# Half-size products in the third block from the end, and vector sums moved between stages, in a retention and bilinear FFN kernel

## The chip, the cores and the metric

The kernel runs on one core of a Trainium2 chip, as one launch. The time is the device time of that launch in microseconds; the kernel before takes 318.87 us (median of three runs). A core has five engines that run their own queues of instructions and wait for each other by semaphores: TensorE (PE, with its weight loads shown as PEld), VectorE (DVE), ScalarE (ACT), GpSimd (POOL) and SyncE (SP), which here only starts DMAs. Matmul results land in PSUM, in eight banks of 2 KB for each of 128 partitions; all else on the chip lies in SBUF.

## The reference

Eight batches of eight heads, 576 positions, head size 64: a retention layer (scores with a decay for each head, no softmax), then a bilinear feed-forward layer over all 4608 tokens.

```python
scores = scale * np.matmul(q, k.transpose(0, 1, 3, 2))
gamma = 1.0 - 2.0 ** (-5.0 - np.arange(H, dtype=np.float32))
Dmat = np.where(rel >= 0, gamma[:, None, None] ** rel[None, :, :], 0.0)
attn = np.matmul(scores * Dmat[None], v)
x = attn.transpose(0, 2, 1, 3).reshape(B * S, H * D)   # 4608 x 512
out = ((x @ w_a) * (x @ w_b)) @ w_out                  # 512 -> 1536 -> 512
```

## The kernel before

**Tokens and blocks.** Tokens are handled in 18 pairs of 256 (`NP`; n = 0 to 17) and the FFN in ten blocks that begin at tokens 0, 512, 768, 1024, 1536, 2048, 2560, 3072, 3584 and 4096 (the second and third hold 256, the rest 512, two pairs). Pairs 15 and 17 (`LEFT`) hold the last 64 positions of each batch; the others hold 256 positions of one batch.

**A block has two stages.** In the *layer*, x (transposed, `xT`, 128 partitions by 4 by 512 tokens) is multiplied with the weights w_a and w_b. The 1536 features are 12 rows F of 128. For each F, four matmuls of 512 columns make `pa` (L1387), ACT copies it to `ha` (L1398), four more make `pb` (L1405), and DVE multiplies both into `hT` (L1410). In the *rows* stage `hT` is multiplied with w_out into the output. From token 1536 on (`MIXED`) the rows stage (`rows_mixed`, tiles named `m`, L1045) takes two rows F at a time (a pair p of h rows, six in all) by seven half-size products instead of eight, in the manner of Strassen and Winograd. That needs sums of h rows (`row_sums`, L979, into `hsum` and in place into `hT`) and sums of w_out (`weight_sums`, made once), both on DVE. ACT copies the banks out (`straight`, `crossed`, L1057), POOL adds two of the four output quarters (L1068), and DVE makes `less` (L1078) and from it the other two (L1085), which are the last to read the banks of `m34`.

**Sevens in the layer too.** In the last block, pairs p = 0, 1, 3, 4 of h rows (`SEVENS`) are also taken by seven products in the layer, and in the block before it (3584, `MIDDLE`) pairs 0 and 1. One pair is then 28 matmuls of 256 columns instead of 16 of 512 (`layer_mixed`, L1220, tiles `lm`, `ls`, `la`). They need eight weight sums for p = 0 and 1 together, eight for p = 3 and 4 (`combine`, L1173, tiles `combos` and `combo`), and four sums of x for each block (`combine_rows`, L1190, tile `rows`). ACT copies products out (L1227), DVE adds (L1231), and POOL multiplies the a part with the b part into `hT` (L1232). `ORDER_MIDDLE` is the order of the products by hand; after it come F = 4 to 11 as usual.

**The retention in between.** PE's work is counted in units of one 512-column matmul (0.2155 us). A list `todo` says at which unit of the whole run other work is issued; it is looked at only at an edge, which in a usual layer is the end of each `pb`, and in a layer by sevens comes only when no pair of h rows is under way. A *stretch* (into, outof) issues on PE the key-value products (`kv`) and scores (`sc`) of one pair of tokens and the outputs (`o`, `os`) of the pair before. Two stretches stand in each later block, about 24 and 88 units into the layer. Ahead of them POOL casts and scales q, k, v of a pair (`ahead`, L578 to L615), SP transposes q and k by DMA (`turn`) and loads the pair after the next.

**What follows a stretch.** DVE adds `kv` to the running state in four sums (L690), which free the two banks of `kv`, and masks the scores (L743); ACT converts states and copies the outputs into x. Part of this goes into a list `jobs` with a priority and a cost. `work(budget)` issues from it after each `pb`. `flush` issues all jobs, `settle` only those of the states and masks. `NOW` is how many of the four state sums are issued at the stretch itself; the others are jobs. Row sums have priority 1, weight sums 1.5 and up.

**Banks and buffers.** `pa`, `pb`, `kv`, `os`, `lm` and part of `m` share the four banks of `ps_ffn`; a new tile takes the bank whose last reader comes first in program order. `ls` and `sc` share two banks, `la`, `o` and the rest of `m` two more (one tile). Output tiles `osb` have four buffers; `store_formed` issues the stores of a block's outputs at F = 2 of the next usual layer, or in the last layer.

**Places.** In the kernel before, the weight sums are issued as jobs: p = 0 with w_a in the layer of 2048, with w_b in that of 2560; p = 3 with w_a in that of 3072, with w_b in 3584 (50 units in). The x sums of the next block stand in the rows stage after both `less`.

Of the kernel before, what the change touches and what calls it, by code (L numbers as in the profile page):

```python
# [11 lines left out]
BF16 = mybir.dt.bfloat16  # L12
# [6 lines left out]
def kernel(  # L19
# [10 lines left out]
    nc = tc.nc  # L30
# [4 lines left out]
    NTOK = B * S  # L35
# [9 lines left out]
    NP = NTOK // 256  # L45
# [799 lines left out]

    def stretch(into, outof):

        (settle if into == NP - 1 else flush)()
        if into == FIRST:
            ps_next("pair", 2)  # L850
        if into in LEFT:
            open_outputs(outof, True)
            open_outputs(into)
            masked = matched(into)
            close_outputs(outof)
            later.append(lambda: masked(0))
            later.append(lambda: masked(1))
            return
        if into == 5:
            convert, convert_swapped = keyed(into, False,  # L860
                                             lambda: open_outputs(outof))
            pop()
            pop()
        else:
            if outof is not None and outof not in opened:
                open_outputs(outof)
            convert, convert_swapped = keyed(into, outof is None)
        masked = matched(into)
        if outof is not None:
            close_outputs(outof)  # L870
        if into == 4:
            later.append(later.pop(1))
            behind.extend([lambda: masked(0), convert, lambda: masked(1)])
            behind.extend(convert_swapped(apart=True))
            return
        if into > MIXED:
            for add in later[:NOW]:
                add()
            jobs.extend((0, 0.5, add) for add in later[NOW:4])
            jobs.append((0, 0, lambda: copies_due.extend(  # L880
                [convert, convert_swapped])))
            jobs.extend((0 if into % 2 else 2, 0.7,
                         lambda on=on: masked(on)) for on in (0, 1))
            copies_due.extend(later[4:])
            later.clear()
            return
        later.append(lambda: (convert(), masked(0)))
        later.append(lambda: (convert_swapped(), masked(1)))
# [116 lines left out]
    def rows_mixed(tok0, hT, sums):  # L1005
# [118 lines left out]
                yield from product(g, 1, part, g == 0)  # L1124
        work(math.inf)
        pass_on(math.inf)
        for g in (0, 1):
            yield from cross(g)
            lessen(g)
        if tok0 + 512 in MIDDLE or pair[1] == NP - 3:  # L1130
            for i in range(4):
                combine_rows(tok0 + 512, i)
        for g in (0, 1):
            for way, *end in ends:
                yield from product(g, way, range(NP2), False)
# [4 lines left out]

    SEVENS = (0, 1, 3, 4)
    COMMON = (0, 1)
    SHARED = 0
    combos = {}

# [3 lines left out]
            "p c (q e f) -> p e c q f", e=2, f=128)  # L1149
        return [[w[:, e, c:c + 2] for c in (0, 2)] for e in (0, 1)]  # L1150

    def combine(p, m, i):

        if (p, m) not in combos:
            shape = [128, 4, 2, 2, 128]
            if p in COMMON:
                if m == 0:
                    both = late["combo"].tile([128, 2] + shape[1:], BF16,
                                              tag="combo", name="combos")
                    combos[p, 0], combos[p, 1] = both[:, 0], both[:, 1]  # L1160
            else:
                combos[p, m] = stage.tile(shape, BF16, tag=("qf", "kf")[m],
                                          name="combo")
            for own in (0, 1):
                if (p, own) in combos:
                    combos[p + 1, own] = combos[p, own]
        (a11, a12), (a21, a22) = quarter_weights(m, p, 2)
        s3, s1, s2, s4 = (combos[p, m][:, k] for k in range(4))
        out, one, other, op = [(s3, a11, a21, ALU.subtract),
                               (s1, a21, a22, ALU.add),  # L1170
                               (s2, a22, s3, ALU.subtract),
                               (s4, a12, s2, ALU.subtract)][i]
        jobs.append((1.5 + i / 10, 0.5, lambda: nc.vector.tensor_tensor(  # L1173
            out, one, other, op=op)))

    row_combos = {}

# [76 lines left out]

        return quarter, after

    MIDDLE = (NTOK - 1024,)
    ORDER_MIDDLE = (
        (1, 0), (2, 0), (1, 1), (6, 0), (5, 0), (6, 1), (7, 0), (3, 0),
        (5, 1), (2, 1), (4, 0), ("a", 4), (3, 1), (7, 1), ("b", 4),  # L1260
# [4 lines left out]
    def middle_layer(tok0, xT, hT, sums):  # L1265

        quarter, after = layer_mixed(tok0, xT, hT)
        has, underway = {}, set()
        for way, at in ORDER_MIDDLE:
            if way in ("a", "b"):  # L1270
                F = at
                p1 = ps_ffn.tile([128, 512], FP32, tag="ab", name="p" + way)
                for c in range(NC):
                    w = wa_sb if way == "a" else wb_sb
                    nc.tensor.matmul(p1, w[:, c, F * 128:F * 128 + 128],  # L1275
                                     xT[:, c], start=(c == 0),
                                     stop=(c == NC - 1))
                    if c < NC - 1:
                        yield 1, False
                if way == "a":  # L1280
                    pop()
                    pass_on(1)
                    if F == 2:
                        store_formed()
                    has[F] = ha_pool.tile([128, 512], BF16, tag="ha",
                                          name="ha")
                    nc.scalar.copy(has[F], p1)
                    yield 1, False
                    continue
                nc.vector.tensor_tensor(hT[:, F], has[F], p1, op=ALU.mult)  # L1290
                pop()
                done, last = F // 2 if F % 2 else None, 1
            else:
                if way == 1:
                    underway.add(at)
                yield from quarter(at, way)
                after(at, way)
                if way == 4:
                    underway.remove(at)
                done, last = at if way == 4 else None, 0  # L1300
            if done is not None and done % 2:
                jobs.extend(row_sums(hT, sums, done - 1, done + 1))
            if done == 5:
                while later:
                    pop()
                work(math.inf, 1)
            work(SHARE_MIDDLE[way])
            yield last, way in ("b", 4) and not underway
# [298 lines left out]
    for n in range(8, NP, 2):  # L1607
# [19 lines left out]
             (411.95, store_held, (2,)), (412.3, load_pair, (11, (K, V))),  # L1627
             (458, load_pair, (12,)), (447, store_held, (2,)),
             (456, store_held, (2,))]
    NOW = 2  # L1630
    LATE = 8, 8, 8, 50, 8
    CAST_A, TURN_A, CAST_B, TURN_B = 96, 58, 96, 58
    for n in range(11, NP):
        casts[n] = placed[n] - (CAST_A if n % 2 else CAST_B)
        turns[n] = placed[n] - (TURN_A if n % 2 else TURN_B)
    for fn, places in ((ahead, casts), (turn, turns)):
        todo += [(at, fn, (n,)) for n, at in places.items()]
    for i in range(16):
        todo.append((starts[NP - 10 + 2 * (i // 4)] + LATE[i // 4]
                     + i % 4 * LATE[4], combine,  # L1640
                     (SEVENS[i // 8 * 2], i // 4 % 2, i % 4)))
    todo.sort(key=lambda e: e[0])

    at = 0.0
# [40 lines left out]
```

## Time and profile before

| | |
|---|---|
| runs | 318.87 us median of 3 (318.01 to 318.91) |
| profiled execution | 318.54 us, of which the span of its instructions is 316.8 |
| layer of block 1536 | 121.6 to 145.1 in the span |
| rows stage of 1536 | 145.1 to 154.4 |
| rows stage of 2048 | 178.6 to 187.9 |
| rows stage of 2560 | 211.9 to 221.1 |
| rows stage of 3072 | 244.2 to 253.2 |
| rows stage of 3584 | 275.2 to 284.2 |
| layer of 4096 | 284.2 to 303.7 |
| its rows stage and the end | 303.7 to 316.8 |

The profile is of one execution. In a timeline, a row gives the start in us from the span's start, the duration of the group, the engine, the line of the program, the operation, the tile that it writes and those that it reads, its shape and how many instructions are merged in the row; in brackets stands the idle time of the engine before the group and what ended it. Matmuls overlap, so that a group of four with 512 columns lasts 1.03 us though the next one can start 0.86 after it. Some matmul records are missing; a group then shows x3.

### The profile page before, as it was taken

Reading aid. Unit: us, or ns where it says so; the run is one execution under the profiler, and the core shown is the slowest. Engines: PE = TensorE matmul, PEld = TensorE weight load, DVE = VectorE, ACT = ScalarE, POOL = GpSimd, SP = SyncE. Lnnn points to the kernel's source line nnn. Section 1 sums busy time; section 2 is a strip of 40 time slices with the busy share of each in tenths; the row PEclk is TensorE's granted clock in tenths of the full one; section 3 lists DMA queues with packets and bytes.
Section 4 is the critical chain, followed back from the end, with each engine's and each line's share of the span. In section 5 each row is a group of like instructions: output and inputs, shape, how many; then the busy total and the mean of one; then the engine's idle time right before and its main releaser. Section 6 shows DMA issues by size and latency. Waiting matters only on the chain.

```text
span 316.8 us, 9373 instructions
## 1 busy us (share of the span) xinstructions
PE 306.2 (97%) x3836; PEld 191.1 (60%) x3871; DVE 218.7 (69%) x426; ACT 151.0 (48%) x339; POOL 169.6 (54%) x187
## 2 busy tenths in 40 slices
PE   8899999999999999999999999999999999999995
PEld 3554457768544554548654774468545875587774
DVE  5845346767857662579568957886678786859873
ACT  6745346526435454444455535444434555335630
POOL 3990068654994568574796069704990340035313
PEclk9999999999999999999999999999999999999999
DMA  8999999999999999999999986983730030004004
GB/s 213 257 203 207 253 231 194 184 211 179 208 178 222 212 216 204 231 223 280 197 256 218 178 218 139 187 185 77 191 59 11 2 132 2 2 0 134 1 3 132
DMA packets 144795, 50.94 MB, mean 161 GB/s; under 512 B 126576, under 2 KB 141680, under 8 KB 144752
## 3 DMA queue, kind: packets, MB, share of 16 engines
q1 hardware_dynamic: 138272, 45.10, 70.3%
q0 software_dynamic: 5808, 4.72, 9.5%
q8 instruction: 30, 0.49, 0.7%
q10 hardware_dynamic: 672, 0.52, 0.5%
q14 instruction: 13, 0.11, 0.1%
HBM read 37.75 MB, written 9.44 MB: 149 GB/s over the span
## 4 chain that ended last, share of the span: by engine, by line
PE 88%; DVE 3%; issue 2%; DMA 2%; SPq 2%; ACT 2%; DVEq 0%
PE pb L1405 21%; PE pa L1387 20%; PE m L1045 17%; PE po L1431 7%; PE lm L1220 3%; PE pa L1275 2%; PE pb L1275 2%; DMA qf<-in_q_dram 2%; SPq L182 2%; PE ls L1220 2%; PE po L931 2%; PE sc L734 1%; PE o L762 1%; PE o L775 1%; PE kv L663 1%
## 5 line engine op out<-in xcount | busy, mean ns | idle before, releaser
L1410 DVE TENSOR_TENSOR hT<-ha,pb 128x512 bf16<-128x512 bf16 (+1 forms) x96 | 59.3, 618 | 50.0 <-PE pb L1405 43.1
L1405 PE MATMUL pb<-xT,wb_sb 128*128 128x512 bf16 (+1 forms) x382 | 86.9, 352 | 1.0 <-DVE hT L1410 0.7
L1398 ACT CAST ha<-pa 128x512 bf16<-128x512 f32 (+1 forms) x96 | 50.9, 531 | 72.2 <-PE pa L1387 69.5
L1387 PE MATMUL pa<-xT,wa_sb 128*128 128x512 bf16 (+1 forms) x358 | 82.8, 351 | 1.8 <-issue 1.1
L1405 PEld LDWEIGHTS <-wb_sb 128*128 128x128 bf16 x384 | 37.4, 98 | 36.6 <-issue 2.1
L1387 PEld LDWEIGHTS <-wa_sb 128*128 128x128 bf16 x376 | 35.8, 98 | 32.7 <-issue 0.3
L1068 POOL TENSOR_TENSOR osb<-crossed,straight 128x512 f32<-128x512 f32 x12 | 15.2, 1269 | 73.3 <-ACT crossed L1057 53.9
L615 POOL TENSOR_TENSOR vb<-vf,vs 128x1024 bf16<-128x1024 f32 (+1 forms) x17 | 29.4, 1731 | 4.1 <-DMA vf<-in_v_dram 1.9
L578 POOL TENSOR_TENSOR qkb<-qf,qs 64x1024 bf16<-64x1024 f32 x12 | 23.3, 1941 | 15.4 <-DMA qf<-in_q_dram 15.4
L1045 PEld LDWEIGHTS <-hT 128*128 128x128 bf16 x288 | 28.1, 98 | 4.4
L1431 PE MATMUL po<-wo_sb,hT 128*128 128x512 bf16 x113 | 26.7, 379 | 0.8 <-issue 0.6
L583 POOL TENSOR_TENSOR qkb<-qf,qs 64x512 bf16<-64x512 f32 x24 | 25.4, 1077 | 0.7
L1045 PE MATMUL m<-wo_sums,hsum 128*128 128x256 bf16 x216 | 25.7, 273 | 0.0
L1045 PEld LDWEIGHTS <-hsum 128*128 128x128 bf16 x216 | 21.1, 98 | 2.4
L979 DVE TENSOR_TENSOR hsum<-hT 128x512 bf16<-128x512 bf16 (+2 forms) x51 | 22.1, 462 | 0.4
L690 DVE TENSOR_TENSOR sums<-kv,sums 128x256 f32<-128x256 f32 x44 | 18.6, 422 | 2.2 <-DVE sums L687 0.5
L743 DVE TENSOR_TENSOR sT<-sc,mask 128x512 bf16<-128x512 f32 x30 | 19.8, 682 | 0.0
L608 POOL CAST qkb<-kf 64x512 bf16<-64x512 f32 (+1 forms) x34 | 19.2, 592 | 0.9
L604 POOL CAST qkb<-kf 64x1024 bf16<-64x1024 f32 (+1 forms) x17 | 16.1, 945 | 6.1 <-DMA kf<-in_k_dram 5.3
L1431 PEld LDWEIGHTS <-hT 128*128 128x128 bf16 x120 | 11.2, 98 | 12.4
L1078 DVE TENSOR_TENSOR less<-m,crossed 128x512 f32<-128x512 f32 (+1 forms) x14 | 8.3, 613 | 13.2 <-ACT crossed L1057 13.2
L1045 PE MATMUL m<-wo_sums,hT 128*128 128x256 bf16 x144 | 16.9, 273 | 0.0
(159 smaller groups left out, 442.4 us busy)
## 6 DMA issues: line engine op xcount, KB each, us to landing
qf<-in_q_dram SPq DMA_DIRECT2D x32, 256.0 KB, 4.7
vf<-in_v_dram SPq DMA_DIRECT2D x32, 256.0 KB, 5.3
kf<-in_k_dram SPq DMA_DIRECT2D x31, 256.0 KB, 4.9
out_dram<-osb SPq DMA_DIRECT2D x9, 512.0 KB, 3.9
out_dram<-osb SPq DMA_DIRECT2D x22, 128.0 KB, 2.8
wo_sb<-in_moe_w_out_dram POOLq DMA_DIRECT2D x3, 512.0 KB, 16.1
out_dram<-osb SPq DMA_DIRECT2D x6, 256.0 KB, 3.7
qf<-in_q_dram SPq DMA_DIRECT2D x8, 128.0 KB, 3.7
```

The source lines that it names most:

```text
L578: nc.gpsimd.tensor_tensor(per_head(qkb[0:64, Q]), per_head(t[0:64]), by[0:64].unsqueeze(2).to_broadcast([64, 2 * H, D]), op=ALU.mult)
L583: nc.gpsimd.tensor_tensor(per_head(qkb[64:128, Q])[:, 1 - r::2], per_head(t[64:128])[:, r::2], by[64:128, r::2].unsqueeze(2).to_broadcast( ...
L608: nc.gpsimd.tensor_copy(to[:, :, 1 - r], fro[:, :, r])
L615: nc.gpsimd.tensor_tensor(vb[:, e].rearrange("p (h d) -> p h d", d=D), t[:, e].rearrange("p (h d) -> p h d", d=D), decay[:, at], op=ALU.mult)
L743: nc.vector.tensor_tensor(sT[:, on].rearrange("p c k s -> p (c k) s"), sc[on].rearrange("p c k s -> p (c k) s"), mask3.unsqueeze(1).to_bro ...
L979: lambda e=ways[i]: nc.vector.tensor_tensor(*e[:3], op=e[3]))
L1045: nc.tensor.matmul(to, rows, cols, start=(begins and p == 0), stop=True, skip_group_check=True)
L1387: nc.tensor.matmul(pa[:, 0:n], wa_sb[:, c, fs], xT[:, c], start=(c == 0), stop=(c == NC - 1))
L1398: nc.scalar.copy(ha[:, 0:n], pa[:, 0:n])
L1405: nc.tensor.matmul(pb[:, 0:n], wb_sb[:, c, fs], xT[:, c], start=(c == 0), stop=(c == NC - 1))
L1410: nc.vector.tensor_tensor(hT[:, F, 0:n], has[F][:, 0:n], pb[:, 0:n], op=ALU.mult)
L1431: nc.tensor.matmul(po, hT[:, F, u * 128:(u + 1) * 128], wo_sb[:, F], start=(F == 0), stop=(F == NF - 1))
```

## The change

- Block 3072 (`NTOK - 1536`) joins `MIDDLE`: its pairs 0 and 1 of h rows are taken by seven products in the layer. Its row sums are made in two groups (`GROUPS`), for pairs 0 to 3 and 4 to 5, as in a usual layer; those of 3584 stay in three.
- Weight sums: four are issued straight to DVE in the rows stage of block 1536 and four in that of 2048 (`between`, `AT`), between the products that need no `less` and the last ones; these are all of p = 0. The eight of p = 3 are jobs of block 3584, from 50 units on, eight units apart (`after_these`).
- The sums of x (`combine_rows`) are issued in that same place, ahead of `cross` and `less`; since 3072 is in `MIDDLE`, there are three sets of them instead of two.
- State sums: four at once at a stretch into an odd pair, one into an even pair (`NOW = 1, 4`), instead of two each.
- The stretch into pair 15 calls `settle` instead of `flush`, as the one into pair 17 did.
- The units of `todo` follow, since block 3072 now counts four units less.

```diff
-        (settle if into == NP - 1 else flush)()
+        (settle if into in LEFT else flush)()
...
         if into > MIXED:
-            for add in later[:NOW]:
+            now = NOW[into % 2]
+            for add in later[:now]:
                 add()
-            jobs.extend((0, 0.5, add) for add in later[NOW:4])
+            jobs.extend((0, 0.5, add) for add in later[now:4])
...
         work(math.inf)
         pass_on(math.inf)
+        if tok0 + 512 in MIDDLE or pair[1] == NP - 3:
+            for i in range(4):
+                combine_rows(tok0 + 512, i)
+        for sum_ in between.pop(tok0, ()):
+            combine(*sum_, now=True)
         for g in (0, 1):
             yield from cross(g)
             lessen(g)
-        if tok0 + 512 in MIDDLE or pair[1] == NP - 3:
-            for i in range(4):
-                combine_rows(tok0 + 512, i)
         for g in (0, 1):
             for way, *end in ends:
...
     COMMON = (0, 1)
+    EACH = [(p, m, i) for p in SEVENS[::2] for m in (0, 1) for i in range(4)]
+    AT = (4, 4, 0, 0, 0)
+    between, rest = {}, EACH[:]
+    for t, count in zip(range(256 * MIXED, NTOK - 512, 512), AT):
+        between[t], rest = rest[:count], rest[count:]
+    after_these = {t: [rest.pop(0) for _ in range(min(count, len(rest)))]
+                   for t, count in ((NTOK - 1536, 0), (NTOK - 1024, 8))}
...
-    def combine(p, m, i):
+    def combine(p, m, i, now=False):
...
             if p in COMMON:
-                if m == 0:
-                    both = late["combo"].tile([128, 2] + shape[1:], BF16,
-                                              tag="combo", name="combos")
-                    combos[p, 0], combos[p, 1] = both[:, 0], both[:, 1]
+                both = late["combo"].tile([128, 2] + shape[1:], BF16,
+                                          tag="combo", name="combos")
+                combos[p, 0], combos[p, 1] = both[:, 0], both[:, 1]
...
-        jobs.append((1.5 + i / 10, 0.5, lambda: nc.vector.tensor_tensor(
-            out, one, other, op=op)))
+        def made():
+            nc.vector.tensor_tensor(out, one, other, op=op)
+
+        if now:
+            made()
+        else:
+            jobs.append((1.5 + i / 10, 0.5, made))
...
-    MIDDLE = (NTOK - 1024,)
+    GROUPS = ((0, 4), (4, 6)), ((0, 2), (2, 4), (4, 6))
+    MIDDLE = (NTOK - 1536, NTOK - 1024)
...
-            if done is not None and done % 2:
-                jobs.extend(row_sums(hT, sums, done - 1, done + 1))
+            for p0, p1 in GROUPS[MIDDLE.index(tok0)]:
+                if done == p1 - 1:
+                    jobs.extend(row_sums(hT, sums, p0, p1))
...
-    NOW = 2
-    LATE = 8, 8, 8, 50, 8
+    NOW = 1, 4
+    LATE = 8, 50, 8
...
-    for i in range(16):
-        todo.append((starts[NP - 10 + 2 * (i // 4)] + LATE[i // 4]
-                     + i % 4 * LATE[4], combine,
-                     (SEVENS[i // 8 * 2], i // 4 % 2, i % 4)))
+    for t, sums_ in after_these.items():
+        todo += [(starts[t // 256] + LATE[t == NTOK - 1024] + LATE[2] * i,
+                  combine, sum_) for i, sum_ in enumerate(sums_)]
```

## The prediction, made before the changed kernel ran

> **What bounds the kernel now.** I read the page first, for the engines and the chain that ended last; then the stretches of the last blocks side by side; then TensorE's (PE's) timeline for holes; then what VectorE (DVE) and GpSimd (POOL) did around each hole.
>
> ```profile
> span 316.8 us, 9373 instructions
> PE 306.2 (97%) x3836; PEld 191.1 (60%) x3871; DVE 218.7 (69%) x426; ACT 151.0 (48%) x339; POOL 169.6 (54%) x187
> ```
>
> PE is busy 97% of the span, so a change pays only if PE has less to do or waits less. The stretches below are four layers (the first half of a block: x times w_a and w_b, then the product). Columns: length, then busy time and count for PE, weight load, DVE, ACT and POOL, then PE's granted clock.
>
> ```profile
> core 0: us, PE busy (x) PEld busy (x) DVE busy (x) ACT busy (x) POOL busy (x), PEclk, DMA share, GB/s
> 154.40:178.60 24.20, 23.46 (x343) 11.73 (x346) 17.89 (x30) 11.55 (x23) 16.82 (x15) 1.00 1.22 219
> 187.90:211.90 24.00, 23.24 (x342) 11.69 (x345) 19.00 (x30) 11.15 (x22) 15.54 (x14) 1.00 0.98 192
> 221.10:244.20 23.10, 22.78 (x311) 11.38 (x313) 17.14 (x26) 9.41 (x21) 15.81 (x14) 1.00 0.38 93
> 253.20:275.20 22.00, 21.84 (x280) 13.19 (x282) 16.89 (x36) 11.21 (x25) 4.24 (x6) 1.00 0.13 49
> ```
>
> They are the layers of blocks 2048, 2560, 3072 and 3584. The clock is 1.00 throughout. 3072 is the one that changes; 3584 already has two pairs of h rows by seven products, so it is the pattern. All four are PE-bound, but the first two are longer than their work. Where PE waited is seen in its timeline, where each group of four 512-column matmuls should start 0.86 after the one before:
>
> ```profile
> 131.52 1.03 PE L1387 MATMUL pa<-xT,wa_sb 128*128 128x512 bf16 x4
> 132.53 1.02 PE L1405 MATMUL pb<-xT,wb_sb 128*128 128x512 bf16 x4
> ...
> 162.55 1.03 PE L1387 MATMUL pa<-xT,wa_sb 128*128 128x512 bf16 x4
> 163.56 1.02 PE L1405 MATMUL pb<-xT,wb_sb 128*128 128x512 bf16 x4
> ...
> 171.33 1.03 PE L1387 MATMUL pa<-xT,wa_sb 128*128 128x512 bf16 x3
> 172.67 1.02 PE L1405 MATMUL pb<-xT,wb_sb 128*128 128x512 bf16 x4 [0.32 <-DVE hT L1410]
> ...
> 195.88 1.03 PE L1387 MATMUL pa<-xT,wa_sb 128*128 128x512 bf16 x4
> 197.29 1.02 PE L1405 MATMUL pb<-xT,wb_sb 128*128 128x512 bf16 x4 [0.39 <-DVE hT L1410]
> ```
>
> Start to start less 0.86 gives waits of 0.15, 0.15, 0.48 and 0.55, in all 1.33 us. Each is a pb that needs a PSUM bank which DVE's product hT has not freed. DVE's and then POOL's timeline tell why:
>
> ```profile
> 162.82 0.69 DVE L1410 TENSOR_TENSOR hT<-ha,pb 128x512 bf16<-128x512 bf16 x1 [1.00 <-PE pb L1405]
> ...
> 169.30 2.73 DVE L1173 TENSOR_TENSOR combos<-wa_sb,combos 128x512 bf16<-128x512 bf16 x2
> 171.95 0.67 DVE L1410 TENSOR_TENSOR hT<-ha,pb 128x512 bf16<-128x512 bf16 x1
> ...
> 193.69 2.09 DVE L1173 TENSOR_TENSOR combos<-wb_sb 128x512 bf16<-128x512 bf16 x1
> 196.56 0.68 DVE L1410 TENSOR_TENSOR hT<-ha,pb 128x512 bf16<-128x512 bf16 x1
> ```
>
> ```profile
> 193.60 1.90 POOL L615 TENSOR_TENSOR vb<-vf,vs 128x1024 bf16<-128x1024 f32 x1
> 195.46 2.08 POOL L578 TENSOR_TENSOR qkb<-qf,qs 64x1024 bf16<-64x1024 f32 x1
> ```
>
> The two long waits end with an hT that stood behind weight sums (L1173). Such a sum is held while POOL multiplies: the one at 193.69 ends at 195.78, 0.28 after POOL's product, though POOL's next product had come up at 195.46. The two short ones come just after a stretch: the state sums still hold the banks of kv, two sums made at once and two after the next hT, so the second pb gets the bank that hT (162.82 to 163.51) has just left.
>
> **The change part by part.** *Sevens in block 3072.* For pairs 0 and 1, 32 matmuls of 512 columns become 56 of 256. Their prices stand in the chain of waits, one run of each kind:
>
> ```profile
> 244.22 9.17 PE m L1045 x84
> ...
> 260.92 0.86 PE pa L1275 x4
> ```
>
> That is 0.109 each against 0.2155: 56 x 0.109 = 6.10 for 32 x 0.2155 = 6.90, so -0.80, all of it on PE, the engine that sets the end. The layer of 3584, where the same 56 stand in the same order, is 1.1 shorter than that of 3072, part of which is its smaller second stretch; so the gain is there, and lies under 1.1. The products wait in places for ACT's copies of one another, so I take -0.7, with bounds of -0.5 and -0.8.
>
> *Weight sums out of the layers.* The eight of pairs 0 and 1 leave the layers of 2048 and 2560, where they made the waits 0.48 and 0.55. The other eight go to block 3584, after most of its layer; 3072 loses four. Four now stand in the rows stage of block 1536, ahead of less (L1078), and four in that of 2048. DVE there waits for ACT, in 1536 and in 2048:
>
> ```profile
> 149.98 1.28 DVE L743 TENSOR_TENSOR sT<-sc,mask 128x512 bf16<-128x512 f32 x2
> 152.33 1.29 DVE L1078 TENSOR_TENSOR less<-m,crossed 128x512 f32<-128x512 f32 x2 [1.07 <-ACT crossed L1057]
> 153.54 0.75 DVE L1085 TENSOR_TENSOR osb<-m,less 128x256 f32<-128x256 f32 x2
> ...
> 184.52 0.69 DVE L1078 TENSOR_TENSOR less<-m,crossed 128x512 f32<-128x512 f32 x1 [1.43 <-ACT crossed L1057]
> ...
> 253.39 0.88 DVE L1190 TENSOR_TENSOR rows<-xT,rows 128x512 bf16<-128x512 bf16 x2
> ```
>
> ```profile
> 152.37 2.50 POOL L1068 TENSOR_TENSOR osb<-crossed,straight 128x512 f32<-128x512 f32 x2 [6.32 <-DMA vf<-in_v_dram]
> ```
>
> ```profile
> 156.03 1.03 PE L1387 MATMUL pa<-xT,wa_sb 128*128 128x512 bf16 x4
> ```
>
> A sum of this shape that nobody holds takes 0.44 (253.39, two in 0.88), so four take 1.7. In 1536 they start at 151.26. The fourth starts at about 152.5, when POOL's osb sums run. Left alone they end at 153.0; held by one of the two osb sums, at 152.37 + 1.25 + 0.28 = 153.9; held by both, at 155.15. So less comes 0.6, 1.6 or 2.8 later than 152.33. Queued behind it are the osb sums of L1085, which end at 154.3 and free the bank for PE's pa at 156.03: room of 1.7. The price is thus 0, 0 or 1.1; I take 0, because the sum at 193.69 waited for one product of POOL and not for the next. In 2048, 1.7 against 1.43 moves only the first less. If that cover were gone, the whole 1.7 would lie on the path twice.
>
> *Sums of states at once.* After a stretch into an odd pair all four now run before the next hT, and free both kv banks about 1.7 after the stretch, when PE is in its second group. That takes away the two 0.15. Into an even pair one runs instead of two; the last hT of the layer comes 0.42 earlier. Against it: at an odd stretch hT stands 0.8 later, but its pb has by then only just ended, so nothing.
>
> *Row sums of x (L1190)* move ahead of less, from behind it, and a third set of four is new. They fall in the same kind of gap (1.43). Nothing, with bounds from -0.1 (PE's small waits at the first products by seven) to +0.6 (the first la of the next layer waits for less).
>
> *The stretch into pair 15* can only start between the quarters, 40 units into the layer instead of 24 (a unit is 0.2155). It is followed 44 units, 9.5 us, later by the next. All it needs is made in the block before; nothing. The outputs of block 2560 now go out behind two transposes on SP's queue; their buffers are next written two blocks later; nothing. *settle* instead of flush at that stretch leaves sums waiting that nobody needs yet; nothing.
>
> *What comes new on DVE and POOL in 3072.* Six products of POOL (L1232) stand behind its casts for pair 16, and ahead of those for pair 17:
>
> ```profile
> 220.40 1.90 POOL L578 TENSOR_TENSOR qkb<-qf,qs 64x1024 bf16<-64x1024 f32 x1
> ...
> 226.90 1.90 POOL L615 TENSOR_TENSOR vb<-vf,vs 128x1024 bf16<-128x1024 f32 x1
> ...
> 256.28 0.73 POOL L1232 TENSOR_TENSOR hT<-straight 128x256 bf16<-128x256 f32 x1 [3.54 <-DVE straight L1231]
> ```
>
> Count from the layer's start, 220.9. Pair 16 ends at +7.9, the six (0.73 each) at +12.2; the row sums that read them start after hT of F = 7, at about +15.3 (6.1 for the quarters, eight groups of 0.86, a stretch of some 1.4, and hT's 0.7 with a little behind it). So POOL is early enough by 3 us. But pair 17's 8.4 us now run from +12.2 to +20.6, over the three hsum and two hT sums (L979) of the first four pairs. Before, these ran as follows:
>
> ```profile
> 239.81 0.69 DVE L1410 TENSOR_TENSOR hT<-ha,pb 128x512 bf16<-128x512 bf16 x1 [0.44 <-PE pb L1405]
> ...
> 241.54 0.69 DVE L1410 TENSOR_TENSOR hT<-ha,pb 128x512 bf16<-128x512 bf16 x1 [0.43 <-PE pb L1405]
> 242.14 1.29 DVE L979 TENSOR_TENSOR hT<-hT 128x1024 bf16<-128x1024 bf16 x2
> ```
>
> Undisturbed such a sum takes 0.65. Against a cast it took 1.06, against a product of POOL it waits for the end:
>
> ```profile
> 143.24 1.06 DVE L979 TENSOR_TENSOR hT<-hT 128x1024 bf16<-128x1024 bf16 x1
> ```
>
> ```profile
> 142.23 1.53 POOL L608 CAST qkb<-kf 64x512 bf16<-64x512 f32 x2
> ```
>
> Laid out, the first hsum meets the tail of a product (+0.3), the second a cast (+0.3), the third vb's product (+1.4), the last two none: 2.0 more. DVE has 0.87 free there (0.44 + 0.43) and 0.42 less to add: 1.3. So about 0.6 comes through to PE, as a wait of the rows stage for the last hT, or of the next layer for less. Bounds: 0, if the sums slip between the products, and 5.7, if all five wait as long as 193.69 did (1.4 each, 7.0 less 1.3).
>
> The Trainium skill, page "SBUF — State Buffer", section "SBUF: two separate sides", says that VectorE with two inputs in SBUF and GpSimd take one port pair in turn, each for its whole instruction. By it a cast holds a sum as fully as a product does; the row at 143.24 shows less than that.
>
> *Sum:* -0.7 - 1.33 + 0.6 = -1.4. The profiled execution took 318.54 (span 316.8), which gives 317.1. The runs shown have a median of 318.87, 0.3 above it, and spread from 318.01 to 318.91.
>
> **The rivals.** *Held as fully by casts as by products.* If each sum that finds POOL at work waits for that instruction and then takes its whole 0.65, the three hits cost 0.8, 0.6 and 1.9: 3.3, less 1.3 is 2.0, and 318.5 results, no change. For it speaks 193.69; against it, 143.24 above, and that the sum at 193.69 ended 0.28 after the product. This is what the cited page's rule would give.
>
> *The gap of block 1536 is too short* (both osb sums hold the fourth weight sum): +1.1, 318.2. For it: POOL's two follow each other at once (2.50 for both). Against it: so did those at 193.60 and 195.46, and DVE got in between.
>
> *Row sums held all the way, the one that ends slower.* Place: layer 3072 from F = 7 on. Price 1.4 for each of five sums that waits like 193.69. From three and a half on (4.8 less 1.3 is 3.5, more than the 2.0 gained) it is slower by over 1 us; with five 318.54 - 2.0 + 5.7 = 322.2. For it: pair 17's casts fill the whole stretch. Against it: only three of their instructions there are products.
>
> *The waits go, the sevens give nothing*, or the other way round, because small waits come up at the seams (the change not doing what it says): 318.54 less 0.7 is 317.8, less 1.33 is 317.2.
>
> *Nothing new in 3072:* 318.54 - 2.0 = 316.5, inside the forecast.
>
> **How the numbers follow.** The forecast, 316.2 to 317.7, has 0.66, with 316.5 in it; one part alone 0.12 (317.2 to 317.8); casts as full holders 0.08; the gap of 1536 0.07; held all the way 0.07. About 1 us, 0.3%, is what a measurement can tell here: faster means under 317.9. From the forecast and three quarters of the one-part case come 0.75 faster (its 317.8 is on the border); the rest of it, casts and gap make 0.18 the same; 0.07 slower. The range from 316.0 (the low end of the runs' spread under 316.5) to 318.6 (no change) leaves out the slower case and a tenth at the edges.
>
> **What would show it.** Right: no wait of pb near 132, 163, 172 and 197; the layer of 3072 at 22.4 to 23.0 instead of 23.1, with 56 quarter products at 0.109; the four weight sums in 1536 between the masks and less, and pa at its place. Wrong: holes in PE at the rows stage of 3072 or at the first la of 3584 longer than 1 us, hsum sums of 2 us in 3072, or a pa of block 2048 that waits for osb. The forecast fails most easily in how many of the five row sums POOL holds.

## The result, and the profile after

The changed kernel took 316.45 us (median of 6 runs, 316.29 to 316.76) where the kernel before took 318.47 beside it (median of 6 as well): a ratio of 0.9934, 95% interval 0.9916 to 0.9952. Run a second time it gave 0.9949 (0.9932 to 0.9965). So it is faster by 0.5 to 0.7%, inside the range forecast and 0.65 us under the forecast of 317.1. The profiled execution took 316.43 against 318.54, so 2.1 less.

From the page of the changed kernel, its span and its engines:

```profile
span 314.7 us, 9436 instructions
PE 304.8 (97%) x3861; PEld 193.3 (61%) x3895; DVE 221.3 (70%) x434; ACT 152.4 (48%) x343; POOL 174.7 (55%) x193
```

PE is busy 1.4 us less and idle 0.7 less; POOL has six products more. The same four layers, side by side (columns as before):

```profile
core 0: us, PE busy (x) PEld busy (x) DVE busy (x) ACT busy (x) POOL busy (x), PEclk, DMA share, GB/s
153.83:177.29 23.46, 23.04 (x343) 11.68 (x346) 16.28 (x27) 11.56 (x23) 17.15 (x15) 1.00 1.32 231
186.90:210.40 23.50, 23.13 (x342) 11.73 (x345) 14.52 (x26) 11.07 (x22) 15.36 (x14) 1.00 1.01 199
219.60:242.10 22.50, 22.24 (x335) 13.69 (x337) 15.96 (x26) 10.89 (x25) 20.64 (x20) 1.00 0.30 70
251.10:273.10 22.00, 21.84 (x280) 13.21 (x282) 15.69 (x33) 11.21 (x25) 4.24 (x6) 1.00 0.12 49
```

The layers of 2048 and 2560 lost 0.74 and 0.50, that of 3072 0.60, that of 3584 nothing. In PE's timeline the waits of pb are gone, and another has come:

```profile
131.10 1.03 PE L1403 MATMUL pa<-xT,wa_sb 128*128 128x512 bf16 x4
131.96 1.03 PE L1421 MATMUL pb<-xT,wb_sb 128*128 128x512 bf16 x4
...
170.62 1.03 PE L1403 MATMUL pa<-xT,wa_sb 128*128 128x512 bf16 x3
171.48 1.03 PE L1421 MATMUL pb<-xT,wb_sb 128*128 128x512 bf16 x4
...
177.16 3.06 PE L1046 MATMUL m<-wo_sums,hT 128*128 128x256 bf16 x24
...
194.84 1.03 PE L1403 MATMUL pa<-xT,wa_sb 128*128 128x512 bf16 x4
195.71 1.03 PE L1421 MATMUL pb<-xT,wb_sb 128*128 128x512 bf16 x4
```

Each pb starts 0.86 or 0.87 after its pa, as does the one at 162.85. The 24 products of m at 177.16, the first of the rows stage of 2048, take 3.06; undisturbed they take 2.78. That is a wait of 0.28 which the prediction did not have.

VectorE's timeline at the three places that the prediction priced: the weight sums in the rows stage of 1536, the last hT of 2048's layer, and the row sums of 3072; and GpSimd's at the last of them, the casts and products of pair 17:

```profile
151.02 0.75 DVE L1183 TENSOR_TENSOR combos<-wa_sb 128x512 bf16<-128x512 bf16 x2
151.69 0.88 DVE L1183 TENSOR_TENSOR combos<-wa_sb,combos 128x512 bf16<-128x512 bf16 x2
152.49 1.28 DVE L1079 TENSOR_TENSOR less<-m,crossed 128x512 f32<-128x512 f32 x2
...
177.78 0.69 DVE L1426 TENSOR_TENSOR hT<-ha,pb 128x512 bf16<-128x512 bf16 x1 [1.20 <-ACT xT L833]
...
235.03 0.92 DVE L980 TENSOR_TENSOR hsum<-hT 128x1024 bf16<-128x1024 bf16 x1
...
236.51 0.89 DVE L980 TENSOR_TENSOR hsum<-hT 128x1024 bf16<-128x1024 bf16 x1
...
238.23 0.74 DVE L980 TENSOR_TENSOR hsum<-hT 128x1024 bf16<-128x1024 bf16 x1
...
239.96 1.93 DVE L980 TENSOR_TENSOR hT<-hT 128x1024 bf16<-128x1024 bf16 x2
```

```profile
233.35 2.06 POOL L583 TENSOR_TENSOR qkb<-qf,qs 64x512 bf16<-64x512 f32 x2
235.47 1.38 POOL L604 CAST qkb<-kf 64x1024 bf16<-64x1024 f32 x1
236.89 1.54 POOL L608 CAST qkb<-kf 64x512 bf16<-64x512 f32 x2
238.52 2.22 POOL L615 TENSOR_TENSOR vb<-vf,vs 128x1024 bf16<-128x1024 f32 x1
```

In 1536 the four weight sums run free, 0.4 each. In 3072, the term in doubt: the five row sums take 4.48 instead of 5 x 0.65 = 3.25, so 1.2 more. The third, forecast to be held 1.4 by the product vb, started 0.29 ahead of it and took 0.74; vb waited instead (2.22, where it takes 1.90 alone, at 225.42). The first of the last two, forecast to meet nothing, met the rest of vb: the pair took 1.93 instead of 1.29. The free time forecast was 1.3, and no wait of PE stands behind these sums: the products of m that follow, at 241.96, start 0.86 after the last pb.

### The profile page after: what moved, and what is told of

Read it like the earlier page. It is cut to its first block, busy times and chain, and to the rows that moved or that the text cites. A ratio compares the mean times of both kernels' runs of the same rounds, so it can differ in the third digit from the quotient of the medians.

```text
span 314.7 us, 9436 instructions
## 1 busy us (share of the span) xinstructions
PE 304.8 (97%) x3861; PEld 193.3 (61%) x3895; DVE 221.3 (70%) x434; ACT 152.4 (48%) x343; POOL 174.7 (55%) x193
## 4 chain that ended last, share of the span: by engine, by line
PE 91%; DMA 2%; issue 2%; POOL 1%; SPq 1%; DVE 1%; ACT 1%; DVEq 0%; POOLq 0%
PE pb L1421 19%; PE pa L1403 19%; PE m L1046 17%; PE po L1447 8%; PE lm L1234 5%; PE pa L1290 4%; PE pb L1290 4%; PE ls L1234 2%; DMA vf<-in_v_dram 2%; PE po L932 2%; PE sc L734 1%; PE o L762 1%; PE o L775 1%; PE kv L663 1%; SPq L182 1%
## 5 line engine op out<-in xcount | busy, mean ns | idle before, releaser
L1426 DVE TENSOR_TENSOR hT<-ha,pb 128x512 bf16<-128x512 bf16 (+1 forms) x84 | 51.1, 609 | 46.8 <-PE pb L1421 41.0
L1421 PE MATMUL pb<-xT,wb_sb 128*128 128x512 bf16 (+1 forms) x334 | 74.6, 348 | 0.3
L1403 PE MATMUL pa<-xT,wa_sb 128*128 128x512 bf16 (+1 forms) x314 | 71.0, 347 | 1.4 <-issue 1.0
L1414 ACT CAST ha<-pa 128x512 bf16<-128x512 f32 (+1 forms) x84 | 43.9, 524 | 57.2 <-PE pa L1403 54.7
L1421 PEld LDWEIGHTS <-wb_sb 128*128 128x128 bf16 x336 | 32.8, 98 | 29.6 <-issue 0.3
L1403 PEld LDWEIGHTS <-wa_sb 128*128 128x128 bf16 x328 | 31.3, 98 | 27.3 <-DVE sums L690 0.2
L980 DVE TENSOR_TENSOR hsum<-hT 128x512 bf16<-128x512 bf16 (+2 forms) x51 | 25.6, 531 | 0.5
L1046 PE MATMUL m<-wo_sb,hT 128*128 128x256 bf16 x144 | 16.9, 273 | 0.0
```

What stands on the lines that cost most here:

```text
L980: lambda e=ways[i]: nc.vector.tensor_tensor(*e[:3], op=e[3]))
L1046: nc.tensor.matmul(to, rows, cols, start=(begins and p == 0), stop=True, skip_group_check=True)
L1403: nc.tensor.matmul(pa[:, 0:n], wa_sb[:, c, fs], xT[:, c], start=(c == 0), stop=(c == NC - 1))
L1414: nc.scalar.copy(ha[:, 0:n], pa[:, 0:n])
L1421: nc.tensor.matmul(pb[:, 0:n], wb_sb[:, c, fs], xT[:, c], start=(c == 0), stop=(c == NC - 1))
L1426: nc.vector.tensor_tensor(hT[:, F, 0:n], has[F][:, 0:n], pb[:, 0:n], op=ALU.mult)
```

## The experiments

Twelve more runs were made, one of them of the changed kernel again, each beside the kernel before on the same chip. Ratios are to that kernel, with 95% intervals; spans are of the profiled execution (316.8 before, 314.7 and 314.9 in the two of the changed kernel).

**The sevens of block 3072 alone**, on the kernel before:

```diff
-        (settle if into == NP - 1 else flush)()
+        (settle if into in LEFT else flush)()
...
-    MIDDLE = (NTOK - 1024,)
+    GROUPS = ((0, 4), (4, 6)), ((0, 2), (2, 4), (4, 6))
+    MIDDLE = (NTOK - 1536, NTOK - 1024)
```

> The kernel before with the first part of the change alone: block 3072 takes pairs 0 and 1 by seven products; the weight sums stay in the layers, two state sums at once as before, x sums behind less. Theory (the terms of the prediction are separate): PE loses 32 matmuls of 0.2155 for 56 of 0.109, 0.6 to 0.7 us faster; the four waits of pb (0.15, 0.15, 0.48, 0.55) stay. Rival A (the sevens pay only with the sums moved, since VectorE's layer of 3072 then also carries weight sums beside the new row sums): PE waits in the rows stage of 3072 or at the next la, 0 to 0.3 faster or slower. Rival B (row sums held by GpSimd's pair 17 as the prediction had it): 0.1 faster.

Measured: 322.09 us, ratio 1.0128 (1.0105 to 1.0150), slower by 3.8 us by the medians, span 319.9; outside everything expected. VectorE, POOL and PE at the start of 3072's layer:

```profile
219.10 3.03 DVE L1190 TENSOR_TENSOR rows<-xT 128x512 bf16<-128x512 bf16 x2
222.16 2.34 DVE L1190 TENSOR_TENSOR rows<-xT,rows 128x512 bf16<-128x512 bf16 x2
```

```profile
219.76 2.08 POOL L578 TENSOR_TENSOR qkb<-qf,qs 64x1024 bf16<-64x1024 f32 x1
221.90 2.32 POOL L583 TENSOR_TENSOR qkb<-qf,qs 64x512 bf16<-64x512 f32 x2
```

```profile
223.37 0.61 PE L1220 MATMUL lm<-rows,combos 128*128 128x256 bf16 x4 [1.61 <-DVE rows L1190]
...
225.89 0.60 PE L1220 MATMUL ls<-xT,combos 128*128 128x256 bf16 x4 [0.60 <-ACT less L1227]
...
242.84 1.02 PE L1276 MATMUL pb<-xT,wb_sb 128*128 128x512 bf16 x4 [1.17 <-DVE hT L1291]
```

Behind less, the four x sums run against pair 16's products on POOL and take 5.4 instead of 1.76. By spacing PE waits 1.77 and 0.77 for them. Later it waits 1.33, where hT stands behind four weight sums that still stand in this layer (1.61 and 1.91 for two each, against pair 17's products and casts on POOL) and a row sum that met vb (1.71); and 0.44 at the rows stage, where the last hT stands behind the second of two state sums, which VectorE began only at 247.18, after 0.46 of idleness. Together 4.3, against the 0.6 gained. This part does not pay without the other moves. The 0.48 of the layer of 2048 is not in this profile, though its weight sums stand where they stood: the two at 169.17 met casts and took 1.25, where before they met the product vb and took 2.73. That wait, then, hung on who came first.

**The weight sums alone:** four in the rows stage of 1536, four in that of 2048, eight in 3584, the rest as before.

```diff
+        for sum_ in between.pop(tok0, ()):
+            combine(*sum_, now=True)
         for g in (0, 1):
             yield from cross(g)
```

> The kernel before with the weight sums moved alone: four in the rows stage of block 1536, four in that of 2048, eight in block 3584; sevens in 3584 only, two state sums at once, x sums behind less. Theory: the waits of 0.48 near 172.7 and 0.55 near 197.3 go, the two of 0.15 near 132.5 and 163.6 stay: 1.0 us faster, less whatever the sums cost in the rows stages (0.25 in that of 2048, if the wait seen there after the change is theirs). Rival A (a wait of the bank is only passed on to the next group): under 0.3 faster. Rival B (the 0.55 belongs to the state sums and not to the weight sum, since hT then also stands behind them): 0.5 faster.

Measured: 317.63, ratio 0.9987 (0.9970 to 1.0004), so not to be told from the kernel before; the profiled span is 0.8 less. PE's timeline where the 0.55 was:

```profile
195.37 1.03 PE L1403 MATMUL pa<-xT,wa_sb 128*128 128x512 bf16 x4
196.38 1.02 PE L1421 MATMUL pb<-xT,wb_sb 128*128 128x512 bf16 x4
```

The 0.48 is gone, and of the 0.55 there is 0.15 left (1.01 less 0.86), the wait that the other odd stretches have too. So 0.40 of it went with the weight sum, and 0.15 belongs to the state sums.

**The state sums alone** (`NOW`), on the kernel before:

```diff
-            for add in later[:NOW]:
+            now = NOW[into % 2]
+            for add in later[:now]:
...
-    NOW = 2
+    NOW = 1, 4
```

> The kernel before with the state sums alone changed: four at once at an odd stretch, one at an even one. Theory: the two waits of 0.15 near 132.5 and 163.6 go, 0.48 and 0.55 stay: 0.3 us faster, under what the rounds can tell, so the timeline of PE decides. Rival A (four at once put hT 0.8 later and its pb waits): the waits come back at the next pb, 0 to 0.3 slower. Rival B (the 0.55 near 197 hangs on the state sums too): 0.8 faster.

Measured: 318.81, ratio 1.0020 (1.0005 to 1.0035). The two short waits are gone (the 0.48 was not there either, and the 0.28 of the changed kernel was), but a longer one has come where the 0.55 was:

```profile
192.93 2.10 DVE L1174 TENSOR_TENSOR combos<-wb_sb 128x512 bf16<-128x512 bf16 x1
194.95 1.86 DVE L690 TENSOR_TENSOR sums<-kv,sums 128x256 f32<-128x256 f32 x4
```

```profile
196.41 1.04 PE L1388 MATMUL pa<-xT,wa_sb 128*128 128x512 bf16 x4 [1.13 <-DVE sums L690]
```

All four state sums now stand behind a weight sum that POOL holds, and PE waits 1.29 for the banks of kv. In the changed kernel, with the weight sums out of the way, the same order costs nothing at this place.

**The changed kernel with `NOW = 2, 2`:**

> The changed kernel with two state sums at once at every stretch, as before the change. Theory: the two waits of 0.15 are back (a third may come at the odd stretches of later blocks), 0.3 us slower than the changed kernel, and the wait of 0.25 in the rows stage of block 2048 stays. Rival A (that wait of 0.25 comes of the state sums' new order): it goes, and the time is the changed kernel's. Rival B (with the weight sums gone the two short waits don't come): no difference.

Measured: 317.41, ratio 0.9968 (0.9954 to 0.9981), span 0.5 over that of the changed kernel (0.3 over its second execution). Three pb wait 0.15 (near 132, 163 and 196), the 0.28 in the rows stage of 2048 is not there, and one of 0.31 has come in that of 3072, where the last hT stands behind two state sums:

```profile
241.90 0.94 DVE L690 TENSOR_TENSOR sums<-kv,sums 128x256 f32<-128x256 f32 x2
242.76 0.68 DVE L1305 TENSOR_TENSOR hT<-ha,pb 128x512 bf16<-128x512 bf16 x1
```

```profile
242.09 3.09 PE L1046 MATMUL m<-wo_sums,hT 128*128 128x256 bf16 x24
```

So the row sums of 3072 stay hidden only with the "0.42 less to add" of the prediction.

**The x sums back behind less**, in the changed kernel: the four `combine_rows` after the loop of `cross` and `lessen`.

> The changed kernel with the x sums put back behind less, as before the change, in the rows stages of blocks 2560 and 3072. Theory A (of the prediction): that move is worth nothing, 0 (-0.1 to +0.6). Theory B (of the run of the sevens alone, where the x sums stood behind less, ran against GpSimd's casts of pair 16 and took 3.03 and 2.34 a pair, and PE waited 1.77 and 0.77 at the first products by seven of 3072): 2 to 2.5 slower, all of it at the first products of 3072; in 3584, where GpSimd has no casts there, nothing.

Measured: 319.07, ratio 1.0036 (1.0023 to 1.0050), span 317.2, so 2.5 more. The x sums take 3.03 and 2.34 again, PE waits 1.77 and 0.77 at the same two products of 3072, and at those of 3584 not at all. Theory B held. In the changed kernel, ahead of less, the x sums of 3072 take 2.6, the second two beside POOL's osb sums, and PE does not wait for them:

```profile
215.25 0.75 DVE L1204 TENSOR_TENSOR rows<-xT 128x512 bf16<-128x512 bf16 x2
216.04 1.86 DVE L1204 TENSOR_TENSOR rows<-xT,rows 128x512 bf16<-128x512 bf16 x2
```

**All eight weight sums in the rows stage of 1536** (`AT = 8, 0, 0, 0, 0`):

> The changed kernel with all eight weight sums of pair 0 in the rows stage of block 1536, none in that of 2048. It measures the room of that gap, 1.7 us by the prediction (osb ends 154.3, pa of block 2048 at 156.03). Theory: the first four run free (151.0 to 152.6), the next four against GpSimd's two osb sums, held at 0.4 to 1.5 each; less comes 2 to 3 us later, osb frees the bank for pa 0.5 to 2.5 late: PE waits at the first pa of block 2048, 0.5 to 2.5 slower. Rival (the sums are not held there and the bank isn't what pa needs): 0.

Measured: 324.08, ratio 1.0187 (1.0169 to 1.0205), span 321.5.

```profile
153.01 2.90 DVE L1183 TENSOR_TENSOR combos<-wb_sb 128x512 bf16<-128x512 bf16 x2
155.84 3.31 DVE L1183 TENSOR_TENSOR combos<-wb_sb,combos 128x512 bf16<-128x512 bf16 x2
```

```profile
161.06 1.87 PE L1403 MATMUL pa<-xT,wa_sb 128*128 128x512 bf16 x4 [4.90 <-DVE osb L1086]
```

The first four are free, the next four cost 6.2 instead of 1.8: past the two osb sums they run into pair 12's products on POOL. The place is the one expected, the pa that needs osb's bank; PE's wait there, 5.1 by spacing, is twice the most that was expected. And the wait is not the whole price: the span is 6.8 longer than that of the changed kernel. PE's granted clock is 0.50 from 160.7 to 164.1, and this pa and the next pb take 3.2 (161.06 to 164.27) where two groups take 1.73, 1.5 more.

**Pair 17's casts ahead of POOL's six products** (`casts[17] = casts[16] + 0.1`):

> The changed kernel with GpSimd's casts of pair 17 ahead of its six quarter products of block 3072 instead of behind them. Theory (the prediction's count: the products end 12.2 us after the layer's start and are needed at 15.3, so 3 us early): now they end at 20.7; the row sums wait for them, and the last hT and the rows stage with them: 3 to 4 us slower, less what the row sums gain by having no casts beside them (up to 1.2). Rival (the row sums have more room than that, being read only by the rows stage at 22.5): under 1 slower.

Measured: 321.01, ratio 1.0089 (1.0073 to 1.0106), span 319.3.

```profile
240.09 0.69 DVE L980 TENSOR_TENSOR hsum<-hT 128x1024 bf16<-128x1024 bf16 x1 [4.78 <-POOL hT L1246]
```

```profile
241.44 1.86 PE L1290 MATMUL pb<-xT,wb_sb 128*128 128x512 bf16 x4 [2.67 <-DVE hT L1305]
```

The first row sum waits 4.78 for the last product, and PE 2.84 by spacing at this pb, near the count. Here too the granted clock falls to 0.50, from 241.5 to 244.9, and the work from this pb to the next takes 4.19 (241.44 to 245.63) instead of the 2.88 of the changed kernel: 1.3 more. So the layer is 4.15 longer (219.81 to 246.49 against 219.43 to 241.96), a little beyond the 3 to 4 expected. Another 0.49 came up in the rows stage of 1536, as it does in the next kernel, which has the casts in their old order. "Early by 3 us" was right (3.6 in the changed kernel, 231.45 to 235.03), and the order on POOL is worth 2.8 of waiting and 1.3 of slower clock.

**Two state sums at the stretch into pair 12 alone** (`NOW[into % 2] + (into == 12)`):

> The changed kernel with two state sums at once, as before the change, at one stretch alone, that into pair 12 (in block 2048's layer), and one at the other even ones. There PE waits 0.28 in the rows stage of 2048 in the changed kernel and in the run of the state sums alone, not in the two runs with two at once. Theory: the wait hangs on that order; it goes, 0.28 faster than the changed kernel. Rival (its hT stands behind a second state sum instead): the same.

Measured: 316.58, ratio 0.9959 (0.9946 to 0.9972), not to be told from the changed kernel. The wait in the rows stage of 2048 is still 0.28, now in two pieces of 0.15 and 0.13, and one of 0.49 stands in that of 1536. The rival held, though with 0.28 at stake the times could not show it; the timeline does.

**Block 2560 by sevens as well**, and its weight sums two blocks earlier: the first four in the rows stage of 1024, the others in that of 1536, the x sums in that of 2048. Besides, in every layer by sevens the stores of earlier outputs now go out at F = 6 instead of 2.

```diff
-    for t, count in zip(range(256 * MIXED, NTOK - 512, 512), AT):
+    for t, count in zip((1024, *range(256 * MIXED, NTOK - 512, 512)), AT):
...
+    GROUPS = ((0, 4), (4, 6)), ((0, 4), (4, 6)), ((0, 2), (2, 4), (4, 6))
+    MIDDLE = (NTOK - 2048, NTOK - 1536, NTOK - 1024)
...
-                    if F == 2:
+                    if F == 6:
                         store_formed()
...
+            if u == 1 and tok0 in between:
+                pools_mixed()
+                for sum_ in between.pop(tok0):
+                    combine(*sum_, now=True)
```

> The changed kernel with a third block, 2560, taking pairs 0 and 1 by seven products; its x sums stand in the rows stage of 2048 ahead of less, its stretch into pair 13 at 40 units; the first four weight sums go from the rows stage of 1536 to that of 1024, where VectorE is idle 3.2 us (111.5 to 114.8) and GpSimd 5.5 (108.2 to 113.7), the other four from 2048 to 1536. Theory: the same trade as in 3072, 0.6 to 0.7 faster than the changed kernel, if the x sums have as much room in the rows stage of 2048 as in that of 2560. Rival A (first products of 2560 wait for the x sums, as they did for those behind less): 1 to 2.5 slower than the changed kernel. Rival B (row sums of 2560 held by GpSimd, since pair 14's casts now run against them, and no cover left): 0 to 0.6 slower.

Measured: 315.86, ratio 0.9916 (0.9890 to 0.9942), span 314.1; the changed kernel on the same chip 316.66 and 314.9. No wait of PE over 0.1 is left in any layer or rows stage from 100 us on, that of 0.28 included. Its layer of 2560 (columns as before), then VectorE and ACT at the last hT of 2048, and the x sums ahead of 2560:

```profile
186.90:209.80 22.90, 22.53 (x368) 14.10 (x370) 17.87 (x30) 12.56 (x26) 20.75 (x20) 1.00 0.94 184
```

```profile
177.94 0.69 DVE L1426 TENSOR_TENSOR hT<-ha,pb 128x512 bf16<-128x512 bf16 x1 [0.93 <-PE pb L1421]
...
182.66 0.75 DVE L1204 TENSOR_TENSOR rows<-xT 128x512 bf16<-128x512 bf16 x2
183.45 1.87 DVE L1204 TENSOR_TENSOR rows<-xT,rows 128x512 bf16<-128x512 bf16 x2
```

```profile
177.48 0.59 ACT L833 CAST xT<-o 128x512 bf16<-128x512 f32 x1
```

22.9 against 23.5, the trade of 3072 once more, and the x sums have the room they had there. By its median it is the fastest kernel of the study; the two intervals overlap.

**The same with two state sums at the stretches into pairs 10 and 12:**

> The kernel with 2560 by sevens, and two state sums at once at the stretches into pairs 10 and 12, one at the later even ones. Theory: the waits in the rows stages of 1536 (0.49 in two of the profiles) and 2048 (0.28) come where the single state sum lets the row sums start earlier against GpSimd's last product: with two they go, 0.3 to 0.7 faster than the kernel with 2560 by sevens alone. Rival (they are chance of the two engines' phases): the same within 0.3.

Measured: 316.46, ratio 0.9939 (0.9916 to 0.9962), span 313.9. No waits either; as the kernel without it had none, this order shows no gain.

**The changed kernel again**, on the chip of the last two:

> The changed kernel itself, beside the two with 2560 by sevens on one chip, and to see which small waits come back in another profiled execution. Theory: 0.9930 to 0.9960 of before; the waits of pb stay away, that of 0.28 in the rows stage of 2048 is there again, 0.49 in that of 1536 may come. Rival (all small waits are chance): neither.

Measured: 316.66, as given above. The waits of pb stay away, that of 0.28 is there again (0.281), the 0.49 is not. So the 0.28 belongs to the kernel, while the 0.49, seen in two other profiles, comes and goes.

**Block 2048 by sevens too**, on the kernel with 2560 by sevens, with all eight weight sums in the rows stage of 1024 and the x sums in that of 1536:

> One block more by sevens, 2048: its x sums in the rows stage of 1536 ahead of less, where the weight sums were; all eight weight sums of pair 0 in the rows stage of 1024, four in each of VectorE's two idle times there (111.7 to 115.0 and 118.6 to 121.5 in the kernel with 2560 by sevens). Theory: the trade of 3072 and 2560 once more, 0.6 to 0.7 faster than that kernel, 315.2, if the x sums end by the time they did in the other rows stages. Rival A (the second four meet GpSimd's product at 120.5, osb goes out late and PE waits): 0 to 1 slower. Rival B (row sums of 1536 end later than in other blocks, since GpSimd's last product holds three of them for 2.79, and the x sums behind them meet the osb sums in full): 0.5 to 2.5 slower, at the pa or the first products of 2048.

Measured: 317.36, ratio 0.9978 (0.9959 to 0.9997): slower than the kernel without it. PE waits 0.78 at the first la of 2048 (for less, behind the x sums) and 0.15 once. Further on, in a block that this edit does not touch, it waits 0.51 and 0.18:

```profile
238.32 2.35 DVE L980 TENSOR_TENSOR hsum<-hT 128x1024 bf16<-128x1024 bf16 x1
```

```profile
238.23 1.90 POOL L615 TENSOR_TENSOR vb<-vf,vs 128x1024 bf16<-128x1024 f32 x1
```

```profile
241.33 1.02 PE L1290 MATMUL pb<-xT,wb_sb 128*128 128x512 bf16 x4 [0.35 <-DVE hT L1305]
```

Here the third row sum of 3072 came 0.09 behind vb and took 2.35, where in the changed kernel it came 0.29 ahead and took 0.74. This is the layout that the prediction had priced at 0.6; it cost 0.69.

## Why the prediction was right, and where it was not

*The four waits, -1.33: right, and more entangled than told.* All four are gone. But they were attributed one cause each, and the 0.55 had two (0.40 and 0.15). The 0.48 is less sure than the others: in both runs that left the weight sums in that layer (sevens alone, state sums alone) it was absent too, so its loss may in part be a matter of who came first. The rival in which one part alone pays was worked out as a plain subtraction, 317.8 and 317.2. The runs of single parts show that parts don't add: sevens alone +3.8 us, state sums alone +0.5, weight sums alone -0.7 by the medians (an interval that holds no change), all together -2.0.

*Sevens, -0.7: right,* with 0.60 inside its bounds of 0.5 and 0.8. The layer is 0.60 shorter in 3072 and 0.60 in 2560 when that block gets them.

*+0.6 for row sums held by POOL: the term that was mis-sized, with its mechanism in place.* The step that failed is "the third vb's product (+1.4)": in the changed kernel that sum came first, the five cost 1.2 more instead of 2.0, and the 1.3 of free time covered that. The price itself, 1.4 for a sum that waits like the one at 193.69, was low: that sum of 128x512 takes 0.44 alone and took 2.09, so it was held 1.65, and with 2048 by sevens the third row sum was held 1.70. And "the last two none" was wrong: the first of them met vb. Without the term of 0.6 the sum is 316.5, next to the 316.45 measured, but that match is luck in part: the sevens gave 0.1 less than forecast, a wait of 0.28 came that nobody forecast, and 0.4 of the gain lies ahead of the first wait (see the last point). The run with block 2048 by sevens shows the forecast's case happening, the one with two state sums at once how little free time was left.

*"The row at 143.24 shows less than that" was a misreading.* The prediction took it as evidence that a cast holds a sum less than a product does. The starts and ends say otherwise. The casts at 142.23 took 1.53 for two, so the second ended at 143.76; the sum that came at 143.24 ended at 144.30, 0.54 later. In the changed kernel the sum at 235.03 ended 0.54 after the product before it (235.41), the one at 236.51 ended 0.55 after the cast (236.85). With 2048 by sevens the one at 238.32 ended 0.54 after vb (240.13). Cast or product makes no difference: what counts is how much of POOL's instruction is still to run when the sum comes up. The rival "casts hold as fully" had the right mechanism with the wrong hits (0.8, 0.6 and 1.9 for three sums; measured 0.27, 0.24 and 0.09, and 0.64 for the last two together); it did not foresee that the third sum would come before vb.

The Trainium skill, page "SBUF — State Buffer", section "SBUF: two separate sides", says that of a VectorE instruction with two inputs in SBUF and a GpSimd one that reads SBUF, whichever starts first has the shared port pair for its whole instruction. The trace agrees, in both directions: each of these sums ended after POOL's instruction, and the cast at 235.47 took 1.38 instead of the 1.03 it takes at 223.07, with a sum running until 235.95.

*Weight sums in the rows stage of 1536 at no cost: right.* Four fit, eight cost 5.1.

*The x sums, "nothing": right for what was done, wrong as a price of the move.* PE does not wait for them in the gap, though they take 2.6 there instead of 1.76. Had they been left in their old place, the third set would have cost 2.5 (measured both ways). The prediction compared with block 3584, where POOL has no casts at that point; in 3072 it has.

*POOL early by 3 us: right;* the reversed order makes PE wait 2.84 and the layer 4.15 longer.

*State sums at an even stretch:* the last hT of the layer was to come 0.42 earlier. In 3072 it did, and was needed. In 2048, hT started at 177.78, 1.49 after its pb (176.29) instead of the usual 1.13, and m waited 0.28. The profile names ACT's copy of xT as what it waited for. Yet with 2560 by sevens, in the same order on VectorE, hT started at 177.94, 1.14 after its pb (176.80), while that copy ran until 178.07. So the copy is not what it needs, and the cause stays open. Of the -2.1, waits and sevens make -1.33 - 0.60 + 0.28 = -1.65. The other 0.4 was there at 131 us (pa at 131.10 for 131.52), ahead of the first wait; the second execution of the changed kernel had 0.17 by then (131.35). So part of it at least is the spread between executions.

## What to carry to other kernels

Price the parts of a change with one another and not one by one: a move that looks like nothing may be what makes the paying part possible, here 2.5 us for four sums moved ahead of a wait. Where VectorE and GpSimd both read and write SBUF, lay their instructions side by side by start and end: here a sum of two SBUF tiles cost what was left of GpSimd's instruction, so that 0.4 us in its start (0.29 ahead of vb or 0.09 behind it) decided over 1.6. A gap has an edge: four sums were free in it, the next four cost 6.2 instead of 1.8 because GpSimd's work begins there. And a long wait of TensorE cost more than its length here: those of 2.84 and 5.1 cost 1.3 and 1.5 more, by the lower clock that came with them.

## What was not expected of the hardware

A sum of 128x1024 that found GpSimd at work ended 0.54 to 0.55 after that instruction's end, in all four cases laid out above, where alone it takes 0.65. GpSimd loses likewise when it comes second: 2.22 for 1.90 and 1.38 for 1.03.

About the end of TensorE's two long waits, 2.84 with pair 17's casts first and 5.1 with all eight weight sums in 1536, its granted clock fell to 0.50 for 3.4 us, and the first group of four products took 1.86 and 1.87 instead of 1.03. Around shorter waits, 1.29 with the state sums alone and 1.77 with the sevens alone, it stayed at 1.00. No run here shows how long a wait must be for that.
